# A segment-recurrent attention layer, forward and backward: folding the output projection's partial sums by block transposes on VectorE, and moving one row-maxima step behind a copy

## The chip, the cores and the metric

The kernel runs on one core of a Trainium2 chip. Its engines are named as in the profile: PE is TensorE (PEld is its weight load), DVE is VectorE, ACT is ScalarE, POOL is GpSimd, and SP is SyncE, which only waits and issues DMAs. The metric is the time of one execution on the device in microseconds, the median of several runs; lower is better.

## The reference

One layer computes `x + s * g`. With `xn = layernorm(x)` (2048 rows of 640), `g` is a gated feed-forward block, and `s` is a recurrent attention: the rows go in 64 segments of 32, and each segment sees 8 memory rows that are the attention output of the segment before.

```python
def _A_ref(x, mem0, Wq, Wk, Wv, Wo, seg_len):      # x 2048x640, 32 heads of 128, 8 memory rows
    mem = mem0
    outs = []
    for s in range(n_seg):                          # 64 segments
        xs = x[:, s * seg_len:(s + 1) * seg_len, :].copy()
        h = jnp.concatenate([mem, xs], axis=1)
        q, k, v = (jnp.einsum('btd,dhe->bhte', h, W) for W in (Wq, Wk, Wv))
        scores = jnp.einsum('bhqe,bhke->bhqk', q, k) * scale
        p = _softmax(jnp.where(mask[None, None], scores, -1000000000.0), axis=-1)
        o = jnp.einsum('bhqk,bhke->bhqe', p, v)
        o = jnp.einsum('bhte,hed->btd', o, Wo)
        mem = o[:, :M, :].copy()
        outs.append(o[:, M:, :])
    return jnp.concatenate(outs, axis=1)

xn = _layernorm(x)
out = x + _A_ref(xn, ...) * _silu(_B_ref(xn, w1, w3, w2))
_out, _vjp = jax.vjp(...)                           # the kernel returns out and the gradients of all nine inputs
```

The memory rows make the forward a chain of 64 steps, and the gradient of the memory rows makes the backward another one, from the last segment to the first.

## The kernel before, in words

The program goes through phases one after the other on one core. Two of them are recurrences, `recurrence` (forward, t = 0 to 63, about 370 to 1,580 us of the span) and `phase4_Abwd` (backward, t = 63 to 0, up to about 2,900 us). Everything around them (the projections of rows that don't depend on the memory, the feed-forward block, the weight gradients) is not touched, except for a few late DMAs.

**A step of a recurrence.** `chain(t, gap)` writes the work that depends on the step before. Between its links it calls `gap("W0")`, `gap("G1")` and so on; `FILL` (forward) and the inner `gap` (backward) put in work that doesn't hang on the chain: the full attention of earlier segments, taken three segments (a tile of 96 rows and 24 memory rows) at a time, in units of four heads (`qd`). A tile has eight units, spread over three steps as 3, 3 and 2 (`SPL`). So a forward step with t mod 3 = 0 or 1 holds three units and one with t mod 3 = 2 holds two; the first three steps hold none. `WARM` adds dummy matmuls of 128x512 at the end of some gaps. The order on each engine is exactly the written order: `in_order` ties every instruction to the one before it on its engine.

**The chain forward.** `hx` (128 x 5 x 32) holds the step's input, turned: features on partitions, five blocks of 128, and 32 columns, of which 0 to 7 are the memory rows and 8 to 31 rows that ride along. From it come K, Q and V (L306), the memory rows' scores and softmax (L647 to L674), and PV (L682), whose result is copied to `oTm` by DVE (L684) and ACT (L685). Then `packed_out` (L317) multiplies by Wo: four groups of rows of one PSUM bank (`pm`, 32 partitions each, tile positions 0, 32, 64, 96) take half of the heads (index a) and half of the 640 output columns (index b) each, so that four matmuls of 32 columns of weights run side by side. Group 2a + b holds columns 320 b to 320 b + 319, summed over the heads of half a. So the two halves over a have to be added, and the result turned back into `hx` for the next step:

- `fold_add` (L330): ACT copies partitions 64 to 127 to SBUF (`fup`, L334), DVE adds them to partitions 0 to 63 in two instructions of 160 columns (`fsum`, L336).
- `fold_turn` (L346): six PE matmuls with a selection matrix as their moving operand turn `fsum` into a PSUM bank (L352).
- a DVE copy to columns 0 to 7 of the next step's `hx` (L699 forward, L1283 backward).
- the rows are stored for later: `FS[t]` forward (a POOL DMA, L700), `GWO` backward (`fold_store`, two POOL DMAs, L343).

The next step's first matmul (Wk forward, WoT backward) waits for `hx`.

Backward, `packed_out` is called for three weights (WvT, WkT, WqT) that accumulate in the same bank, and only then the fold.

**The softmax of the units, forward.** In G2 the scores of the step's units are made (L777 to L782) and unit one's row maxima are taken (`soft_max`: L790 on DVE, then L794). In G3 come unit one's first exponentials on ACT (L812) and unit two's row maxima on DVE; both stand in front of the chain's `oTm` copies on their engines. In G4 follow the other exponentials, unit three's maxima, the products with 1/Z (`norm`: L831 on DVE, L832 on POOL) with the store of each unit's probabilities right after it (L833, a POOL DMA). In G5 and G6 PE transposes the normalised probabilities of units one and two (`turn_p`, L840), DVE copies them (L841), and unit three's `norm` follows.

**Queues.** DMAs issued from SP and from POOL stand in the written order on their engine, and each waits there for its data. SP carries nearly all loads and many stores.

Of the kernel before, what the change touches and what calls it, by code (L numbers as in the profile page):

```python
# [9 lines left out]
BF16 = mybir.dt.bfloat16  # L10
# [6 lines left out]
P = 128  # L17
# [23 lines left out]
class K:  # L41
# [109 lines left out]
    def setup_dram(self):  # L151
# [21 lines left out]
        self.FS = mk("FS", (T, 64, 320))  # L173
# [143 lines left out]
def packed_out(k, pm, x, W, first, last, i0=0, i1=16):  # L317

    nq = x.shape[2]
    for i in range(i0, i1):  # L320
        for a in range(2):
            for b in range(2):
                h = 16 * a + i
                p0 = 32 * (2 * a + b)
                k.nc.tensor.matmul(pm[p0:p0 + nq, 0:320], x[:, h, :], W[:, h, 320 * b:320 * b + 320],  # L325
                                   start=(first and i == 0), stop=(last and i == 15),
                                   tile_position=(0, p0), skip_group_check=True)


def fold_add(k, pm, pool, tag="fup"):  # L330

    fs = pool.tile([64, 320], BF16, name="fsum", tag="fsum")
    up = pool.tile([64, 320], F32, name="fup", tag=tag)
    k.nc.scalar.copy(up[:], pm[64:128, 0:320])  # L334
    for c in (0, 160):
        k.nc.vector.tensor_tensor(fs[:, c:c + 160], pm[0:64, c:c + 160], up[:, c:c + 160], ALU.add)  # L336
# [9 lines left out]
def fold_turn(k, bank, fs):  # L346

    pt = bview(bank, P, k.DC, 8)
    for (dc, p0, c0, w, b) in ((0, 0, 0, 128, 0), (3, 0, 64, 128, 1), (2, 64, 0, 64, 1), (1, 0, 128, 128, 0),
                               (4, 0, 192, 128, 1), (2, 0, 256, 64, 0)):  # L350
        kw = {} if w == 128 else dict(tile_position=(0, p0))
        k.nc.tensor.matmul(pt[p0:p0 + w, dc, :], fs[:, c0:c0 + w], k.sel[0:64, b, :], start=True, stop=True,  # L352
                           skip_group_check=True, **kw)
    return pt
# [200 lines left out]
def recurrence(k, W0, W4, Wv, Wk_, Wq, Wo, own, ps, banks):  # L555
    nc, tc = k.nc, k.tc
    D, DC, S, H, HD, T = k.D, k.DC, k.S, k.H, k.HD, k.T
    with tc.tile_pool(name="achain", bufs=1) as ch, \
# [5 lines left out]
        WARM = dict(G2=1, G3=2, G5=2)  # L564
# [33 lines left out]
        def chain(t, gap):  # L598
# [100 lines left out]
            nc.vector.tensor_copy(nxt[:, :, 0:8], pt[:])  # L699
            nc.gpsimd.dma_start(k.FS[t], fs[:])  # L700
            gap("G6")
# [121 lines left out]
        def norm(tl, qd, eng=nc.gpsimd, q=nc.gpsimd):  # L823
            n = k.geo(tl)[3]
            h0 = qd * 4
# [6 lines left out]
            eng.tensor_tensor(Pb[0:n, :, 0:n], Pb[0:n, :, 0:n], bc_last(rz[0:n], n), ALU.mult)  # L832
            q.dma_start(k.PR[tl][:, h0:h0 + 4, :], Pb[0:n])  # L833
# [84 lines left out]
        def FILL(g, t, at, kbatch):  # L918
# [164 lines left out]
def phase4_Abwd(k, out2, W0, W4, WT, own, ps, banks):  # L1083
# [7 lines left out]
    for s in range(3):  # L1091
        t0 = (2, 0, 1)[s]
        n = (T - 1 - t0 + 2) // 3
        tl0 = 1 if s == 0 else 0
        for b in range(2):
            dst = k.HRO[120 * tl0:120 * tl0 + 120 * (n - 1), :].rearrange("(t r) d -> t r d", r=120)[:, 96 + 8 * s:104 + 8 * s]
            cols = slice(320 * b, 320 * b + 320)
            later.append((dst[:, :, cols], k.FS[t0:t0 + 3 * (n - 1):3, 32 * b:32 * b + 8, :]))
            t1 = t0 + 3 * (n - 1)
            later.append((k.m_rows(k.HRO, t1 + 1)[:, cols], k.FS[t1, 32 * b:32 * b + 8, :]))  # L1100
    for b in range(2):
        later.append((k.SR[0:24 * k.NO, 320 * b:320 * b + 320].rearrange("(t r) c -> t r c", r=24),
                      k.FS[k.OT0:k.OT0 + k.NO, 32 * b + 8:32 * b + 32, :]))
    with tc.tile_pool(name="gst", bufs=1) as st, tc.tile_pool(name="gchain", bufs=1) as ch, \
# [79 lines left out]
        def chain(t, gap):  # L1184
# [93 lines left out]
            fs = fold_add(k, pm, ch, "gstg")  # L1278
            gap("G4")
            if t > 0:  # L1280
                pt = fold_turn(k, bC, fs)
                gap("G5")
                nc.vector.tensor_copy(goxs[(t - 1) % 2][:, :, 0:8], pt[:])  # L1283
            fold_store(nc.gpsimd, k.m_rows(k.GWO, t - 1) if t > 0 else out2f, fs)
# [1007 lines left out]
```

## Time and profile before

| what | value |
|---|---|
| median of 3 runs | 4698.83 us (4696.4 to 4703.39) |
| profiled execution, its own time | 4684.61 us |
| its span, first to last instruction | 4682.7 us |
| first to last fold, forward | 389 to 1,568 us, 63 folds |
| first to last turned fold, backward | 1,824 to 2,882 us, 63 folds |
| DMA share forward (450 to 1,560 us) | 0.59 |
| DMA share backward (1,824 to 2,880 us) | 0.71 |
| L334 ACT copy of 64x320 | 422 ns, x127 |
| L336 DVE add of 64x160 | 311 ns, x254 |
| L352 PE, six matmuls a fold | 177 ns each, x756 |
| L699 and L1283 DVE copy to `hx` | 199 ns, x126 |

The profile is one execution. Its page gives the busy time of each engine, then groups of instructions with their mean duration, the idle time in front of them and what ended it. A group is written as line, engine, operation, what it writes `<-` what it reads, and its count. A row of the timeline has the start in us from the span's start, the duration in us, engine, line, operation and operands, and in brackets how long the engine was idle before it and what released it; `x64` means that many instructions of one kind in a row, merged. Two instructions that are merged can overlap, so their sum is longer than the row.

### The profile page before, as it was taken

The numbers are of one execution on the slowest core, as the hardware profiler recorded it, in microseconds if no ns is written. First come the engines' busy times: TensorE is split into PE (matmuls) and PEld (weight loads), VectorE is DVE, ScalarE is ACT, GpSimd is POOL, SyncE is SP. The second block draws the span as 40 slices with busy tenths as digits, with TensorE's granted clock in tenths as the row PEclk, the third lists the DMA queues.
The fourth block names the chain that finished last, engine by engine and source line by source line (L and its number), as shares of the span: only waits on it lengthen the run. The fifth ranks groups of instructions, "written<-read, shape, count | busy, mean of one in ns | idle before, by whom it ended". The sixth has DMA issues, their size and how long they took to land. (4 is left out here: it accounts for less than half of the span.)

```text
span 4682.7 us, 159785 instructions
## 1 busy us (share of the span) xinstructions
PE 4466.5 (95%) x64504; PEld 2821.1 (60%) x64504; DVE 2244.7 (48%) x7156; ACT 1587.4 (34%) x4360; POOL 2098.4 (45%) x3528
## 2 busy tenths in 40 slices
PE   8999999999999898999999998999999999999999
PEld 4544555555555555666666665676667666666675
DVE  8734666666666534555555553343224432311460
ACT  5432555555544433333333332232223322200000
POOL 6532555555555423455444444354335533311440
PEclk9999999999999998999999999999999999999999
DMA  8773566666655677777777775664345543579783
GB/s 269 236 252 119 175 178 178 179 179 179 180 168 167 167 181 230 211 225 207 215 211 209 208 209 154 144 163 132 110 116 158 147 129 107 170 223 207 159 181 100
DMA packets 976843, 834.77 MB, mean 178 GB/s; under 512 B 518890, under 2 KB 858286, under 8 KB 974144
## 3 DMA queue, kind: packets, MB, share of 16 engines
q1 hardware_dynamic: 763879, 547.92, 42.2%
q0 software_dynamic: 129952, 228.13, 16.4%
q10 hardware_dynamic: 82275, 48.52, 4.0%
q8 instruction: 509, 8.34, 0.8%
q14 instruction: 228, 1.87, 0.1%
HBM read 472.66 MB, written 310.33 MB: 167 GB/s over the span
## 5 line engine op out<-in xcount | busy, mean ns | idle before, releaser
L1667 PE MATMUL wg<-gr,hr 128*128 128x512 bf16 x2400 | 521.7, 379 | 0.0
L1648 PE MATMUL g<-land,ghacc 128*128 128x320 bf16 x3072 | 459.9, 300 | 0.8
L1667 PEld LDWEIGHTS <-hr 128*128 128x128 bf16 x2400 | 233.9, 98 | 278.9
L306 PEld LDWEIGHTS <-hx 128*32 128x32 bf16 x10240 | 246.8, 96 | 229.1 <-issue 14.6
L1648 PEld LDWEIGHTS <-ghacc 128*128 128x128 bf16 x3072 | 289.2, 98 | 104.2 <-ACT ghacc L92 2.2
L90 DVE CAST wgo<-wg 128x512 bf16<-128x512 f32 x72 | 49.8, 692 | 471.2 <-PE wg L1667 471.2
L90 DVE CAST stg<-bank 128x512 bf16<-128x512 f32 x256 | 177.1, 692 | 158.6 <-PE bank L306 154.5
L880 POOL DMA_DIRECT2D OR<-xv x163 | 89.8, 551 | 361.1 <-ACT xv L92 338.5
L1613 POOL DMA_DIRECT2D GSP<-grs x48 | 25.5, 542 | 473.1 <-ACT grs L1605 472.0
L92 ACT COPY ghacc<-t6g 128x768 bf16<-128x768 bf16 (+1 forms) x176 | 137.1, 779 | 293.8 <-PE t6g L1630 284.5
L1324 POOL DMA_DIRECT2D VTD<-gvT x176 | 129.4, 742 | 218.7 <-ACT gvT L1323 209.5
L325 PEld LDWEIGHTS <-gkv 128*8 128x8 bf16 x8192 | 177.6, 86 | 82.2 <-issue 4.1
L832 POOL TENSOR_TENSOR xP<-xP,xrz 120x480 bf16<-120x480 bf16 x163 | 161.1, 988 | 76.0 <-DVE xrz L831 46.6
L812 ACT ACTIVATE xP<-xsp,xnm 120x120 bf16<-120x120 f32 (+1 forms) x540 | 186.1, 372 | 26.0 <-DVE xnm L794 25.9
L1654 DVE TENSOR_TENSOR ghacc<-ghacc,g 128x320 f32<-128x320 f32 x192 | 93.6, 487 | 209.9 <-PE g L1648 209.9
L336 DVE TENSOR_TENSOR fsum<-bank,fup 64x160 bf16<-64x160 f32 x254 | 69.5, 311 | 258.5 <-ACT fup L334 255.2
L92 ACT CAST wgo<-wg 128x512 bf16<-128x512 f32 x48 | 28.1, 585 | 479.8 <-PE wg L1667 407.0
L1371 POOL DMA_DIRECT2D GXP<-gks x157 | 91.0, 580 | 189.5 <-ACT gks L1369 188.8
L325 PE MATMUL bank<-Wo,oTm 128*32 128x320 bf16 x4032 | 154.2, 307 | 18.4 <-DVE oTm L684 18.4
L325 PE MATMUL bank<-WkT,gkv 128*8 128x320 bf16 x4096 | 162.8, 299 | 4.2 <-issue 2.2
L325 PE MATMUL bank<-WvT,gkv 128*8 128x320 bf16 x4096 | 166.4, 305 | 0.5 <-DVE gkv L1197 0.5
L306 PE MATMUL bank<-Wq,hx 128*32 128x512 bf16 x2560 | 161.6, 381 | 0.0
(389 smaller groups left out, 10916.1 us busy)
## 6 DMA issues: line engine op xcount, KB each, us to landing
QVS<-stg SPq DMA_DIRECT2D x128, 256.0 KB
kT<-VTD SPq DMA_DIRECT2D x64, 320.0 KB
PR<-xP POOLq DMA_DIRECT2D x168, 120.0 KB, 3.1
VTD<-gvT POOLq DMA_DIRECT2D x168, 120.0 KB, 4.0
land<-DSR SPq DMA_DIRECT2D x168, 120.0 KB
land<-PR SPq DMA_DIRECT2D x168, 120.0 KB
OR<-xv POOLq DMA_DIRECT2D x163, 120.0 KB, 3.0
orr<-OR SPq DMA_DIRECT2D x14, 1280.0 KB
```

What stands on the lines that cost most here:

```text
L90: return nc.vector.tensor_copy(out, in_)
L92: return nc.scalar.copy(out, in_)
L306: k.nc.tensor.matmul(bank[32 * g:32 * g + 32, :], x[:, dc, :], W[:, dc, c0:c0 + 512], start=(dc == 0), stop=(dc == k.DC - 1), tile_positio ...
L325: k.nc.tensor.matmul(pm[p0:p0 + nq, 0:320], x[:, h, :], W[:, h, 320 * b:320 * b + 320], start=(first and i == 0), stop=(last and i == 15), ...
L812: nc.scalar.activation(Pb[0:n, j, 0:n], sp[0:n, j, :], ACT.Exp, bias=nmx[0:n, j:j + 1], scale=k.scale, accum_out=Z[0:n, j:j + 1])
L832: eng.tensor_tensor(Pb[0:n, :, 0:n], Pb[0:n, :, 0:n], bc_last(rz[0:n], n), ALU.mult)
L880: q.dma_start(k.OR[120 * tl:120 * tl + n, c0:c0 + 512], v[0:n])
L1324: nc.gpsimd.dma_start(k.VTD[tl][:, :, h0:h0 + 4, :], vTq[:])
L1371: (nc.sync if (tl, qd) in pro else nc.gpsimd).dma_start(k.GXP[tl, :, qd, 0:ns], ks[:].rearrange("p s i h m -> p s i (h m)"))
L1648: nc.tensor.matmul(pg[:], ring[:, i, j, r0:r0 + P], Ws[qd][i][:, j, 320 * h:320 * h + 320], start=(i == 0 and j == 0), stop=(i == 2 and j ...
L1654: nc.vector.tensor_tensor(a, a, pg[:], ALU.add)
L1667: nc.tensor.matmul(pw[:], hr[:, tl, dc * P:(dc + 1) * P], grs[i][:, tl, :], start=(tl == 0), stop=(tl == NF - 1))
```

## The change

The two output column halves are no longer 320 wide blocks but interleaved blocks of 32: the columns are taken as 20 blocks of 32, and group b gets every second one. Each matmul still has 320 columns, read from the weights as ten runs of 32.

`fold_add` and `fold_turn` become one function `fold`. ACT copies partitions 64 to 127 in two halves (the even and the odd ones of the group's ten blocks), and DVE adds each half, the even one to partitions 0 to 63 and the odd one to partitions 64 to 127 of a tile of 128 x 160. With this arrangement a transpose of every 32x32 block (one DVE instruction over 128 x 160) leaves features on partitions and rows on columns, in the order that `hx` has; a DVE copy takes the 8 memory columns of each block to `hx`. The six matmuls go, and with them the use of bank C.

`FS` changes from (T, 64, 320) to (T, 32, D). The stores of FS and GWO go from POOL to SP and become four DMAs each, of runs of 32 columns (64 bytes); forward, the store of FS stands behind the loads of gap G5. The late copies out of FS (`later`) become nine DMAs instead of sixteen.

In the forward, gap G6 is merged into G5, so that unit two's transposes and unit three's `norm` follow G5's work, and one WARM matmul of G5 is dropped, the other stands behind them. Unit two's row maxima move from G3 to the head of G4, behind the `oTm` copy. The store of unit one's probabilities moves behind unit two's product.

```diff
-        self.FS = mk("FS", (T, 64, 320))
+        self.FS = mk("FS", (T, 32, D))
...
     for i in range(i0, i1):
         for a in range(2):
+            h = 16 * a + i
+            w = W[:, h, :].rearrange("p (j b r) -> p b j r", b=2, r=32)
             for b in range(2):
-                h = 16 * a + i
                 p0 = 32 * (2 * a + b)
-                k.nc.tensor.matmul(pm[p0:p0 + nq, 0:320], x[:, h, :], W[:, h, 320 * b:320 * b + 320],
+                k.nc.tensor.matmul(pm[p0:p0 + nq, 0:320].rearrange("p (j r) -> p j r", r=32), x[:, h, :], w[:, b],
                                    start=(first and i == 0), stop=(last and i == 15),
                                    tile_position=(0, p0), skip_group_check=True)
...
+def fold(k, pm, pool, dst, tag="fup"):
+
+    ft = pool.tile([P, 2, 160], BF16, name="fsum", tag="fsum")
+    fs, tr = ft[:, 0], ft[:, 1]
+    up = pool.tile([64, 2, 160], F32, name="fup", tag=tag)
+    v = pm[:, 0:320].rearrange("p (c s r) -> p s c r", s=2, r=32)
+    rows = lambda ap: ap.rearrange("p (c r) -> p c r", r=32)
+    for s in range(2):
+        k.nc.scalar.copy(rows(up[:, s]), v[64:128, s])
+        k.nc.vector.tensor_tensor(rows(fs[64 * s:64 * s + 64]), v[0:64, s], rows(up[:, s]), ALU.add)
+    if dst is not None:
+        k.nc.vector.transpose(tr, fs)
+        k.nc.vector.tensor_copy(dst, tr.rearrange("p (c m) -> p c m", m=32)[:, :, 0:8])
     return fs
...
 def fold_store(eng, dst, fs):
 
-    for b in range(2):
-        eng.dma_start(dst[:, 320 * b:320 * b + 320], fs[32 * b:32 * b + 8, :])
+    n = dst.shape[0]
+    d = dst.rearrange("m (c g r) -> g m c r", g=4, r=32)
+    for g in range(4):
+        eng.dma_start(d[g], fs[32 * g:32 * g + n, :].rearrange("m (c r) -> m c r", r=32))
...
-        WARM = dict(G2=1, G3=2, G5=2)
+        WARM = dict(G2=1, G3=2, G5=1)
...
             packed_out(k, pm, oTm, Wo, True, True)
-            fs = fold_add(k, pm, ch)
+            fs = fold(k, pm, ch, hxs[(t + 1) % 2][:, :, 0:8])
             gap("G5")
-            pt = fold_turn(k, bC, fs)
-            nxt = hxs[(t + 1) % 2]
-            nc.vector.tensor_copy(nxt[:, :, 0:8], pt[:])
-            nc.gpsimd.dma_start(k.FS[t], fs[:])
-            gap("G6")
+            fold_store(nc.sync, k.FS[t], fs)
...
-            q.dma_start(k.PR[tl][:, h0:h0 + 4, :], Pb[0:n])
+            if q is not None:
+                norm_store(tl, qd, q)
+
+        def norm_store(tl, qd, q=nc.gpsimd):
+            n = k.geo(tl)[3]
+            q.dma_start(k.PR[tl][:, 4 * qd:4 * qd + 4, :], xPs[qd % 3][0:n])
...
             elif g == "G3":
                 at(lambda a, b: soft_exp(a, b, 0, 2), t, 0)
+            elif g == "G4":
                 at(soft_max, t, 1)
-            elif g == "G4":
                 at(lambda a, b: soft_exp(a, b, 2, 4), t, 0)
                 at(lambda a, b: soft_max(a, b, True), t, 2)
-                at(norm, t, 0)
+                at(lambda a, b: norm(a, b, q=None), t, 0)
...
                 at(soft_exp, t, 1)
-                at(norm, t, 1)
+                at(lambda a, b: norm(a, b, q=None), t, 1)
+                for i in range(2):
+                    at(norm_store, t, i)
                 at(soft_exp, t, 2)
             elif g == "G5":
...
-            elif g == "G6":
                 at(turn_p, t, 1)
                 at(norm, t, 2)
...
-            fs = fold_add(k, pm, ch, "gstg")
+            fs = fold(k, pm, ch, goxs[(t - 1) % 2][:, :, 0:8] if t > 0 else None, "gstg")
             gap("G4")
-            if t > 0:
-                pt = fold_turn(k, bC, fs)
-                gap("G5")
-                nc.vector.tensor_copy(goxs[(t - 1) % 2][:, :, 0:8], pt[:])
-            fold_store(nc.gpsimd, k.m_rows(k.GWO, t - 1) if t > 0 else out2f, fs)
+            gap("G5")
+            fold_store(nc.sync, k.m_rows(k.GWO, t - 1) if t > 0 else out2f, fs)
             gap("G6")
```

More of the change, by code (lines that the diff above doesn't have):

```diff
@@ L327, in packed_out @@
                                    tile_position=(0, p0), skip_group_check=True)
[L330 to L336, printed above, removed]
+def fold(k, pm, pool, dst, tag="fup"):
[10 more added lines that the diff above has]
+        k.nc.vector.tensor_copy(dst, tr.rearrange("p (c m) -> p c m", m=32)[:, :, 0:8])
@@ L337, in fold_add @@
     return fs
 def fold_store(eng, dst, fs):
-    for b in range(2):
-        eng.dma_start(dst[:, 320 * b:320 * b + 320], fs[32 * b:32 * b + 8, :])
[L346 to L354, printed above, removed]
+    n = dst.shape[0]
@@ L694, in chain @@
             packed_out(k, pm, oTm, Wo, True, True)
-            fs = fold_add(k, pm, ch)
+            fs = fold(k, pm, ch, hxs[(t + 1) % 2][:, :, 0:8])
             gap("G5")
-            pt = fold_turn(k, bC, fs)
-            nxt = hxs[(t + 1) % 2]
-            nc.vector.tensor_copy(nxt[:, :, 0:8], pt[:])
-            nc.gpsimd.dma_start(k.FS[t], fs[:])
-            gap("G6")
+            fold_store(nc.sync, k.FS[t], fs)
         WT = {}
@@ L824, in norm @@
             n = k.geo(tl)[3]
-            h0 = qd * 4
             Pb = xPs[qd % 3]
@@ L1094, in phase4_Abwd @@
         tl0 = 1 if s == 0 else 0
[L1095 to L1103, printed above, removed]
+        dst = k.HRO[120 * tl0:120 * tl0 + 120 * (n - 1), :].rearrange("(t r) d -> t r d", r=120)[:, 96 + 8 * s:104 + 8 * s]
+        later.append((dst, k.FS[t0:t0 + 3 * (n - 1):3, 0:8, :]))
+        t1 = t0 + 3 * (n - 1)
+        later.append((k.m_rows(k.HRO, t1 + 1), k.FS[t1, 0:8, :]))
+    later.append((k.SR[0:24 * k.NO, :].rearrange("(t r) c -> t r c", r=24), k.FS[k.OT0:k.OT0 + k.NO, 8:32, :]))
     with tc.tile_pool(name="gst", bufs=1) as st, tc.tile_pool(name="gchain", bufs=1) as ch, \
```

## The prediction

> **What bounds the kernel now.** I read part 1 of the page first, then the groups of instructions, then the timeline of one step of each recurrence, last SP's own instructions.
>
> ```profile
> PE 4466.5 (95%) x64504; PEld 2821.1 (60%) x64504; DVE 2244.7 (48%) x7156; ACT 1587.4 (34%) x4360; POOL 2098.4 (45%) x3528
> ```
>
> PE looks full, but in the two recurrences part of this is filler: WARM matmuls and whatever the gaps put between two links of a chain. What sets a step is that chain, so I look at the end of a step, forward, t = 45:
>
> ```profile
> 1246.97 0.17 DVE L794 TENSOR_SCALAR xnm<-xmx 120x4 f32<-120x4 f32 x1
> 1247.05 0.29 DVE L684 CAST oTm<-bank 128x128 bf16<-128x128 f32 x1
> ...
> 1247.48 2.36 PE L325 MATMUL bank<-Wo,oTm 128*32 128x320 bf16 x64 [0.29 <-DVE oTm L684]
> ...
> 1247.77 0.38 ACT L812 ACTIVATE xP<-xsp,xnm 120x120 bf16<-120x120 f32 x1
> ...
> 1248.33 0.98 POOL L832 TENSOR_TENSOR xP<-xP,xrz 120x480 bf16<-120x480 bf16 x1 [1.36 <-issue]
> ...
> 1249.11 0.62 ACT L808 ACTIVATE xP<-xsp 120x480 bf16<-120x480 f32 x1
> ...
> 1249.94 0.42 ACT L334 COPY fup<-bank 64x320 f32<-64x320 f32 x1 [0.21 <-PE bank L325]
> ...
> 1250.20 1.00 POOL L832 TENSOR_TENSOR xP<-xP,xrz 120x480 bf16<-120x480 bf16 x1
> 1250.40 0.55 DVE L336 TENSOR_TENSOR fsum<-bank,fup 64x160 bf16<-64x160 f32 x2 [0.85 <-ACT fup L334]
> ...
> 1250.77 0.78 PE L352 MATMUL bank<-sel,fsum 64*128 64x8 bf16 x6
> ...
> 1251.49 0.38 PE L840 MATMUL xpp<-ident,xP 120*128 120x120 bf16 x4
> ...
> 1251.59 0.20 DVE L699 CAST hx<-bank 128x40 bf16<-128x40 f32 x1 [0.33 <-PE bank L352]
> ...
> 1251.85 2.34 PE L306 MATMUL bank<-Wk,hx 128*32 128x512 bf16 x40
> ```
>
> Call e the end of the output projection (1247.48 + 2.36 = 1249.84). From e to the next step's first projection are 2.01 us: ACT copy, two adds, six turning matmuls, hx copy. PE fills them, but no link is shortened by that. Backward the same chain stands almost bare (e = 2214.40):
>
> ```profile
> 2214.45 0.42 ACT L334 COPY fup<-bank 64x320 f32<-64x320 f32 x1 [2.26 <-PE bank L325]
> 2214.91 0.55 DVE L336 TENSOR_TENSOR fsum<-bank,fup 64x160 bf16<-64x160 f32 x2 [2.87 <-ACT fup L334]
> ...
> 2215.28 0.78 PE L352 MATMUL bank<-sel,fsum 64*128 64x8 bf16 x6 [0.56 <-DVE fsum L336]
> ...
> 2216.10 0.20 DVE L1283 CAST hx<-bank 128x40 bf16<-128x40 f32 x1 [0.65 <-PE bank L352]
> ...
> 2216.45 1.26 PE L306 MATMUL bank<-WoT,hx 128*32 128x512 bf16 x20
> ```
>
> 2.05 us from e. There are 63 such places in each recurrence, mean periods 18.98 us (389.30 to 1566.13, 62 steps) and 17.03 us.
>
> **What the Trainium skill says.** "VectorE: DVE Perf Modes", section "The three transpose paths", prices a VectorE transpose of 128x128 bf16 at 311 ns, blocks of 32x32 only; the kernel before has none. The same page, "Two Vector instructions with no wait between them", says that an instruction whose output starts in another quadrant of partitions than the last output waits for all earlier ones; today both adds write from partition 0 and overlap (0.55 us for two of 0.311), the new ones write from 0 and from 64, so I take no overlap. "SBUF — State Buffer", "Door 1: The DMA port swizzle", says that reads stay at full bandwidth while successive accesses fall in one 16-byte line; the new projection reads runs of 32 bf16, 64 bytes. The trace agrees as far as it goes: the score matmuls of L782 read three runs of 32 columns and take 202 ns, the contiguous 96-column transposes of L1630 205. The same page, "Who interferes with whom", says that a VectorE copy from SBUF to SBUF in a two-port mode and a GpSimd operation block each other; the DVE copies of L641, which run beside POOL's, have a median of 283 ns and a maximum of 664.
>
> **The change part by part.**
>
> Fold, backward. Gone from the chain are the turning matmuls (first add's end to their end 0.84 us, 2215.22 to 2216.06) and the wait behind them. New: two ACT copies of 64x160. From L334 (422 ns for 320) and the 128x128 copy of L685 (262 ns) ACT pays 0.83 ns an element, so 0.29 each, overlapping by 0.09 as successive ACT operations here do. In us after e: copies 0.05-0.34 and 0.25-0.54, adds 0.37-0.69 and 0.72-1.03 (0.31 each, 0.03 from engine to engine), transpose of 160 columns from 1.06: 0.311 plus 32 more columns at 0.96 GHz, an estimate of 0.345, to 1.41; copy 128x40, 0.19 (today's from PSUM takes 0.199), to 1.63; then 0.14 to the matmul as today (hx ends 2216.30, WoT starts 2216.45): 1.77 against 2.05. 0.27 us x 63 = 17.0. PE holds dprob, one WARM and gmem in the gap, under 1.2 us together, and is free. The DVE work of unit three (L1353 and before) follows the hx copy and moves with it, as do the copies of the next projection. Bounds: a transpose at two elements a cycle (0.26), or half as long again (0.52); a copy of 0.15 to 0.25; that gives 0.05 to 0.40 us, 3 to 25 in all.
>
> Row maxima, forward. L684 starts at e-2.79 behind L790 and L794 of unit two, while PV's matmuls ended at e-3.09; they release a reader in 0.10, so it can start at e-2.99. The other half (ACT L685, 1246.94 + 0.26) ends at e-2.64 and now decides: the projection starts 0.14 earlier, as far behind as today behind L684. The price: unit two's maxima (0.66) and L794 (0.17) come behind the copy. Row maxima end e-1.95, L794 e-1.75, and the exponentials of unit two start at e-1.66 instead of e-2.07; ACT ends L808 at e+0.30 instead of e-0.11.
>
> Fold, forward, same step. fup now waits for ACT and not for PE: copies 0.21-0.50 and 0.41-0.70, adds 0.53-0.85 and 0.88-1.19, transpose to 1.57, copy to 1.79, Wk at 1.85, against 2.01: 0.16. The other route to Wk is unit two's turn (L840), which now stands before it on PE: its 1/Z at 0.16, POOL's product to 1.31 (its neighbour's PR store no longer stands between), transposes 1.37, then 0.22 for them and 0.21 for the one WARM: 1.80, also in time. At t mod 3 = 1 the reduce runs into the copy instead of following 0.09 later, everything is 0.18 sooner, and Wk starts at 1.67 instead of 2.01. At t mod 3 = 2 there is no third unit: PE is free at 1.68, hx ready at 1.60, gain 0.33. With 20 steps of each, 20 x (0.16 + 0.34 + 0.33) = 16.6, and 0.26 for each of the first three: 17.4. Bounds from the same durations: 4 to 27. Unit one's transposes (L840) come late at t mod 3 = 0, at 0.12 instead of -0.07; nothing but filler follows. The WARM that goes (0.21) lies in that filler.
>
> Stores. FS and GWO leave POOL (0.55 and 2 x 0.53 per step) for SP, as four DMAs each of 64-byte runs. SP's similar DMAs of L1273 take 0.63 each, so 2.5 us of SP per step.
>
> ```profile
> 2699.31 0.94 SPq L1311 DMA_DIRECT2D xP<-PR  x1
> 2700.76 0.34 SPq L1215 DMA_DIRECT2D GOS<-gstg  x1
> ...
> 2709.28 1.25 SPq L1273 DMA_DIRECT2D DSR<-dSm  x2
> ```
>
> Backward they go in at 2700.25, where SP has half a microsecond free; the list behind (GOS, three unit loads, VTD, PM, QM, KS) comes some 2 us later and catches up by 2709.28, since SP waits about 0.7 and 0.9 us on the way. SP issues 12.0 us of a 17.0 us step; with these 14.5, with gaps near 16. The loads delayed serve the next step or a later one, over 10 us away: nothing. Forward SP is about half used; the KS store behind is delayed by up to 0.3 us and nobody near waits. The 64-byte packets are small in number beside the rest. Fewer FS reads later (9 for 16 on POOL): nothing. PR's later store: read only backward, nothing.
>
> Sum: 17.0 + 17.4 = 34.4 us. Against the profiled execution's own time, 4684.61 (span 4682.7): 4650.2. The shown runs' median is 4698.83, 14.2 above it; the saving is the same there: 4664.4, so 4664.
>
> **Rivals.**
> A, the softmax gives the forward gain back: exponentials and POOL's product of unit two (0.98 to 1.00 us, started once its 1/Z is there) end later than I reckon and L840 holds Wk. For it: at t mod 3 = 0 the two routes are 0.05 apart. Against: POOL has lost a 0.57 us store in between. Then only the backward gain stays: 4682.
> B, SP is full in the backward: 16 of 17 us, and the gride transposes (1.26 us on SP every fourth step) don't fit. For it: 71% use today. Against: slack of a whole step. If half a microsecond a step is lost, 31 of 34 us go: 4695, no change.
> C, the projection slows with its interleaved columns. L325's 64 matmuls take 2.36 us, 36.9 ns apart, four running at once; b = 0 and 1 now read neighbouring 64-byte runs instead of runs 640 bytes apart. There are 16,320. From 2.1 ns each on (34.4/16,320), the gain is gone; at 3.7 (a tenth) 60 us come on: 4698.83 - 34.4 + 60 = 4724, slower. Against: L782, above.
> D, the hx copy is held by POOL: up to a store's 0.55 us at each of 126 places, 69 us: 4734, slower. Against: the copy starts as POOL's product ends, and L641's median.
>
> **How the numbers follow.** Forecast 0.68, A 0.14, B 0.06, C 0.08, D 0.04. The bounds add up to a gain of 7 to 52 us, 4647 to 4692; since both low ends together are unlikely I close it at 4688, with A inside; B, C, D, 0.18, stay outside. 0.2%, 9.4 us, is what a measurement of this kernel can tell from no change. Faster: forecast and A, 0.82, less a little for their weak end: 0.81. Same 0.08 (B and that end), slower 0.11.
>
> **What would show it.** Right: Wo and WkT matmuls of L325 still 2.36 us for 64; from e to WoT about 1.77 us, to Wk 1.67 to 1.85; the projection 0.14 earlier behind PV; a transpose near 0.345 us and no L352. Wrong: a longer L325; a wait of the hx copy for POOL, or of PE at L840 for POOL longer than at Wk; waits of PE for loads in the backward; a period not below 17.0 us there.

## The result and the profile after

The changed kernel takes 4744.2 us (median of 4 runs, 4732.7 to 4747.5), the kernel before 4701.1 us beside it (4696.4 to 4703.9): a ratio of 1.0088, 95% interval 1.0069 to 1.0108. It is slower by about 0.9%, some 40 us. The profiled execution took 4744.95 us (span 4743.0) against 4684.61 (4682.7).

Where the span grew is read by cutting it at the ends of the output projections (63 folds in each recurrence):

| stretch | before, us | after, us |
|---|---|---|
| start to the first forward fold | 389.3 | 390.1 |
| first to last forward fold (62 steps) | 1176.8 | 1177.9 |
| between the recurrences | 257.7 | 259.8 |
| first to last backward fold (62 steps) | 1056.1 | 1114.5 |
| what is left behind it | 1802.7 | 1800.6 |

All of the loss is in the backward, and in the forward nothing was gained. Part 1 of the page, the line that answers to the first one shown of before:

```profile
PE 4352.1 (92%) x63403; PEld 2768.7 (58%) x63684; DVE 2289.4 (48%) x7282; ACT 1618.4 (34%) x4487; POOL 1980.3 (42%) x3330
```

PE lost 114 us of busy time while the span grew by 60: the turning matmuls and a WARM are gone, and PE now waits more. DVE has 45 us more (transposes, and adds that no longer overlap).

The chain, first backward. The projection ends at e = 2263.18. The timeline of that step (start, duration, engine, line, operation, operands, and in brackets the idle time before it and what ended it):

```profile
2263.23 0.29 ACT L339 COPY fup<-bank 64x160 f32<-64x160 f32 x1 [1.88 <-PE bank L326]
...
2263.55 0.32 DVE L340 TENSOR_TENSOR fsum<-bank,fup 64x160 bf16<-64x160 f32 x1 [2.73 <-ACT fup L339]
...
2263.90 0.29 ACT L339 COPY fup<-bank 64x160 f32<-64x160 f32 x1 [0.38 <-DVE fsum L340]
...
2264.22 0.32 DVE L340 TENSOR_TENSOR fsum<-bank,fup 64x160 bf16<-64x160 f32 x1 [0.35 <-ACT fup L339]
...
2264.57 0.34 DVE L342 STREAM_TRANSPOSE fsum<-fsum 128x160 bf16<-128x160 bf16 x1
...
2264.95 0.17 DVE L343 COPY hx<-fsum 128x40 bf16<-128x40 bf16 x1
...
2265.27 2.34 PE L306 MATMUL bank<-WoT,hx 128*32 128x512 bf16 x40 [1.31 <-DVE hx L343]
```

Every duration is as reckoned to 0.02 us, but copy, add, copy, add run strictly one after the other: the second ACT copy, which needs nothing from DVE, is released by DVE's first add. So WoT starts 2.09 us after e, where it was 2.05.

The step at t = 45, forward, e = 1251.18, in the timeline:

```profile
1248.38 0.29 DVE L682 CAST oTm<-bank 128x128 bf16<-128x128 f32 x1 [0.68 <-PE bank L680]
...
1248.82 2.36 PE L326 MATMUL bank<-Wo,oTm 128*32 128x320 bf16 x64
...
1250.88 0.58 ACT L801 ACTIVATE xP<-xsp 120x480 bf16<-120x480 f32 x1
...
1251.49 0.29 ACT L339 COPY fup<-bank 64x160 f32<-64x160 f32 x1
1251.57 0.98 POOL L824 TENSOR_TENSOR xP<-xP,xrz 120x480 bf16<-120x480 bf16 x1 [0.23 <-issue]
...
1252.16 0.29 ACT L339 COPY fup<-bank 64x160 f32<-64x160 f32 x1 [0.38 <-DVE fsum L340]
...
1252.61 0.38 PE L837 MATMUL xpp<-ident,xP 120*128 120x120 bf16 x4 [0.62 <-POOL xP L824]
...
1253.22 0.17 DVE L343 COPY hx<-fsum 128x40 bf16<-128x40 bf16 x1
1253.45 2.34 PE L306 MATMUL bank<-Wk,hx 128*32 128x512 bf16 x40 [0.45 <-DVE hx L343]
```

The copy `oTm` is now released by PE and not by DVE's row maxima, the projection still takes 2.36 us for 64 matmuls, and unit two's transposes (L837) are done before `hx`. But ACT's exponentials end at e + 0.28, the fold begins at e + 0.31, the same wait for the first add stands inside it, and Wk starts 2.27 us after e (2.01 before).

The backward steps. Most keep a period near 17.03 us, but 12 of the 62 take 19 to 24 us, nine of these right behind a step in which SP also issued a gride transpose (a DMA that loads `gride` turned, L270, every fourth step). SP's own instructions in one of them (a step of 23.0 us, begun at 2605.78) and the end of the step before, from the timeline:

```profile
2594.19 2.99 SPq L352 DMA_DIRECT2D GWO<-fsum  x4
2597.29 1.28 SPq L270 DMA_TRANSPOSE gride<-GS  x1
...
2608.65 1.28 SPq L1267 DMA_DIRECT2D DSR<-dSm  x2
2610.03 0.57 SPq L1168 DMA_DIRECT2D xp<-GXP  x1
2610.70 0.64 SPq L1298 DMA_DIRECT2D kT<-QVM  x1
2611.39 0.61 SPq L265 DMA_DIRECT2D kT<-QVX  x1
2612.09 0.54 SPq L265 DMA_DIRECT2D kT<-GOS  x1
2612.72 0.38 SPq L1302 DMA_DIRECT2D xP<-PR  x1
...
2615.39 2.95 SPq L352 DMA_DIRECT2D GWO<-fsum  x4
2618.45 0.39 SPq L1209 DMA_DIRECT2D GOS<-gstg  x1
```

From 2610.03 on, in the rows left out too, SP goes from one DMA to the next within 0.04 to 0.11 us: it waits for nothing. Four stores and a transpose in the step before have pushed its list back, and the unit loads of this step are issued while the step's own units already stand on PE. The waits of this step (engine and line, what for, us in total, times, longest):

```profile
DVE gOst L1215 <- PE bank L1214: 4.8, 1, 4.8
...
PE gvpt L1311 <- DMA kT<-QVX: 3.5, 1, 3.5
```

PE, which works in written order, stood 3.5 us at a unit's first matmul (L1311, at 2614.68) for the load of QVX that SP issued at 2611.39 and that landed at 2614.63, and the chain's transposes (L1214) stand behind that matmul. Over the whole backward the rows of this wait are:

```profile
PE gvpt L1311 <- DMA kT<-QVS: 18.8, 9, 4.3
PE gvpt L1311 <- DMA kT<-QVX: 10.5, 6, 3.5
```

In the kernel before, PE waits there once, for 0.3 us.

### The profile page after: what moved, and what is told of

The parts are those of the page before. It is cut to its first block, busy times and chain, and to the rows that moved or that the text cites. A ratio compares the mean times of both kernels' runs of the same rounds, so it can differ in the third digit from the quotient of the medians.

```text
span 4743.0 us, 158663 instructions
## 1 busy us (share of the span) xinstructions
PE 4352.1 (92%) x63403; PEld 2768.7 (58%) x63684; DVE 2289.4 (48%) x7282; ACT 1618.4 (34%) x4487; POOL 1980.3 (42%) x3330
## 4 chain that ended last, share of the span: by engine, by line
PE 72%; DVE 9%; DMA 8%; ACT 5%; issue 3%; SPq 1%; POOL 0%; ACTq 0%; DVEq 0%; another core or an unknown queue 0%; POOLq 0%
PE bank L306 11%; PE wg L1658 11%; PE bank L326 11%; PE g L1639 8%; PE oa L1805 4%; PE wa L2193 2%; PE b0pb L364 2%; PE r6p L1589 2%; PE t6g L1621 2%; DVE fsum L340 2%; ACT xP L805 2%; PE pgxb L2126 2%; ACT fup L339 1%; PE bank L1220 1%; PE bank L314 1%
## 5 line engine op out<-in xcount | busy, mean ns | idle before, releaser
L306 PE MATMUL bank<-WoT,hx 128*32 128x512 bf16 x2560 | 153.6, 386 | 91.7 <-DVE hx L343 91.7
L340 DVE TENSOR_TENSOR fsum<-bank,fup 64x160 bf16<-64x160 f32 x254 | 80.5, 317 | 262.2 <-ACT fup L339 260.8
L326 PE MATMUL bank<-WvT,gkv 128*8 128x320 bf16 x4096 | 184.0, 328 | 0.9 <-DVE gkv L1191 0.9
L306 PE MATMUL bank<-Wk,hx 128*32 128x512 bf16 x2560 | 153.1, 386 | 32.2 <-DVE hx L343 31.8
L245 POOL DMA_DIRECT2D land<-GOS x256 | 146.7, 578 | 37.6 <-PE bank L306 9.4
```

The lines of the kernel that those rows point to most:

```text
L245: eng.dma_start(d, src if src.shape[0] > 1 else src[0])
L306: k.nc.tensor.matmul(bank[32 * g:32 * g + 32, :], x[:, dc, :], W[:, dc, c0:c0 + 512], start=(dc == 0), stop=(dc == k.DC - 1), tile_positio ...
L326: k.nc.tensor.matmul(pm[p0:p0 + nq, 0:320].rearrange("p (j r) -> p j r", r=32), x[:, h, :], w[:, b], start=(first and i == 0), stop=(last ...
L340: k.nc.vector.tensor_tensor(rows(fs[64 * s:64 * s + 64]), v[0:64, s], rows(up[:, s]), ALU.add)
```

## The experiments

Two theories. S: the stores of GWO fill SP in the backward, the unit loads come late, and that is the loss. F: the fold costs the time. Inside the fold, two readings of the wait: T, the two copies share a tile; K, ACT and DVE read one PSUM bank and are put in order. In the table, "backward" is the stretch of 62 steps from the first to the last fold of the profiled execution, which is 1056.1 us in the kernel before.

| run | ratio to before | 95% interval | backward, us |
|---|---|---|---|
| changed kernel | 1.0088 | 1.0069 to 1.0108 | 1114.5 |
| GWO stores on POOL | 1.0006 | 0.9999 to 1.0013 | 1063.2 |
| one ACT copy, stores on SP | 1.0085 | 1.0070 to 1.0100 | 1117.8 |
| one ACT copy, stores on POOL | 0.9975 | 0.9965 to 0.9984 | 1051.5 |
| the same, row maxima back in G3 | 0.9967 | 0.9957 to 0.9978 | 1055.1 |
| the same, FS on POOL too | 0.9976 | 0.9968 to 0.9985 | 1056.5 |
| one ACT copy, stores on ACT | 1.0017 | 1.0007 to 1.0028 | 1090.7 |
| two tiles for the copies | 1.0100 | 1.0071 to 1.0129 | 1120.0 |
| two banks forward, stores on POOL | 0.9962 | 0.9952 to 0.9973 | 1064.9 |
| before, 2 GWO stores on SP | 1.0007 | 0.9997 to 1.0018 | 1061.6 |
| before, 4 stores on SP | 1.0029 | 1.0019 to 1.0040 | 1072.8 |
| before, 8 stores on SP | 1.0148 | 1.0131 to 1.0166 | 1138.1 |
| before, row maxima moved alone | 0.9991 | 0.9982 to 1.0000 | 1056.5 |

The kernel before lay at 4696 to 4706 us beside these runs, so runs are compared by their ratios; 0.1% is 4.7 us. A stretch of a single profile varies by some us: the changed kernel and that with two tiles, whose folds take equally long, differ by 6 us forward (1177.9 and 1171.6) and by 5 backward.

**GWO stores back on POOL.**

```diff
-            fold_store(nc.sync, k.m_rows(k.GWO, t - 1) if t > 0 else out2f, fs)
+            fold_store(nc.gpsimd, k.m_rows(k.GWO, t - 1) if t > 0 else out2f, fs)
```

> The changed kernel, with the backward's four GWO stores of a step put back on POOL; fold and forward as changed. Theory S (SP is full in the backward: 2.5 us a step more to issue, unit loads come late): the backward steps of 20 to 23 us go, the 63 backward steps take 1022 to 1028 us in the profile instead of 1079.8, and the time falls by 50 to 60 us, to about 4685 to 4697. Theory F (the fold itself costs the time, SP's delays are hidden): no more than 5 us fall, 4739 to 4746. If POOL in its turn is late with four DMAs, something between.

4698.6 us. The time goes back to that of the kernel before, and the backward falls by 51 us in the profile (the expectation's stretch ends two folds sooner; in it this run took 1028.8 us, 1022.6 before, 1079.8 in the changed kernel). By the ratios the move is worth 0.0082, 39 us; by the two medians, taken at different times, 46. That is short of the 50 to 60 expected, and a few longer steps stay (five over 18 us; three before, 14 in the changed kernel). PE's waits for QVS and QVX at the units' first matmuls are gone as well (none over 0.1 us). So the same four DMAs a step, with the same runs of 64 bytes, don't cost this time when POOL issues them. S holds, F falls: what remains of the whole change with these stores elsewhere is no gain and no loss.

**One ACT copy for both halves.**

```diff
-    up = pool.tile([64, 2, 160], F32, name="fup", tag=tag)
+    up = pool.tile([64, 320], F32, name="fup", tag=tag)
...
+    u = up[:].rearrange("p (c s r) -> p s c r", s=2, r=32)
+    k.nc.scalar.copy(up[:], pm[64:128, 0:320])
...
     for s in range(2):
-        k.nc.scalar.copy(rows(up[:, s]), v[64:128, s])
-        k.nc.vector.tensor_tensor(rows(fs[64 * s:64 * s + 64]), v[0:64, s], rows(up[:, s]), ALU.add)
+        k.nc.vector.tensor_tensor(rows(fs[64 * s:64 * s + 64]), v[0:64, s], u[:, s], ALU.add)
```

> The changed kernel, with one ACT copy of 64x320 in the fold ahead of both adds instead of two halves that alternate with the adds; GWO stores stay on SP. From the durations measured: copy 0.05-0.47 after the projection's end, adds to 1.18, transpose to 1.56, hx copy to 1.77, next matmul at about 1.91 instead of 2.10 backward, and about 2.1 instead of 2.27 forward. If the ACT copy waits for the add because both read one PSUM bank, this gains 0.15 to 0.2 us a fold: forward 9 to 12 us. Backward theory S says that SP sets many steps, so less than the 12 us there: time 4720 to 4738. Theory F (fold alone) says all of 20 to 25: 4719 to 4724, with backward steps as long as before wherever no fold is late.

4732.2 us, a ratio that cannot be told from that of the changed kernel. The trace shows why: forward the stretch of 62 steps fell from 1177.9 to 1165.7 us, about the 9 to 12 us expected. Backward each fold is 0.18 us shorter and the usual steps fell from 17.03 to 16.9 us, but the stretch didn't fall (1117.8 for 1114.5): the long steps, which are there as before (13 over 19 us, 12 in the changed kernel), took the gain.

**Both together.** The two edits above in one kernel.

> Both: one ACT copy, and GWO stores on POOL. Theory S and the bank order together: 60 us from the stores and 20 to 24 from the fold: 4662 to 4685, faster than the kernel before (about 4700). If only the stores matter: 4685 to 4697. If neither: 4740.

4680.6 us, faster than the kernel before, as expected. Against the run with stores on POOL alone the copy is worth 0.0031, 15 us. The backward fold of this kernel in the timeline (e = 2224.16):

```profile
2224.21 0.42 ACT L338 COPY fup<-bank 64x320 f32<-64x320 f32 x1 [1.88 <-PE bank L326]
2224.67 0.67 DVE L341 TENSOR_TENSOR fsum<-bank,fup 64x160 bf16<-64x160 f32 x2 [2.86 <-ACT fup L338]
2225.37 0.34 DVE L343 STREAM_TRANSPOSE fsum<-fsum 128x160 bf16<-128x160 bf16 x1
2225.75 0.17 DVE L344 COPY hx<-fsum 128x40 bf16<-128x40 bf16 x1
2226.07 2.13 PE L306 MATMUL bank<-WoT,hx 128*32 128x512 bf16 x36 [1.12 <-DVE hx L344]
```

WoT at e + 1.91 (expected 1.91), 0.14 before that of the kernel before; the usual periods went from 17.03 to 16.89 us.

**Row maxima put back.** That kernel with unit two's row maxima in G3 again.

```diff
             elif g == "G3":
                 at(lambda a, b: soft_exp(a, b, 0, 2), t, 0)
+                at(soft_max, t, 1)
             elif g == "G4":
-                at(soft_max, t, 1)
```

> As the run with one ACT copy and GWO stores on POOL, but with unit two's row maxima back in G3, in front of the attention output's copy. The trace of the changed kernel shows PV's end to the projection 0.73 to 0.53 us, 0.2 us in 40 steps that have a unit two in them with a turn on the path: 8 to 12 us slower than that run. If the softmax of unit two is what ends the step at t mod 3 = 0, the move gives nothing there: 3 to 6 us. If the move costs more behind the copy than it gains ahead of it: faster by some us.

4678.7 us: not slower by 8 to 12 us, nor by 3 to 6; the two intervals overlap. The timeline at t = 45, first with the maxima moved (e = 1239.94), ACT's queue:

```profile
1239.65 0.58 ACT L802 ACTIVATE xP<-xsp 120x480 bf16<-120x480 f32 x1
...
1240.26 0.42 ACT L338 COPY fup<-bank 64x320 f32<-64x320 f32 x1
```

and with the maxima back in G3 (e = 1245.91):

```profile
1245.19 0.62 ACT L802 ACTIVATE xP<-xsp 120x480 bf16<-120x480 f32 x1
...
1246.02 0.42 ACT L338 COPY fup<-bank 64x320 f32<-64x320 f32 x1 [0.20 <-PE bank L326]
```

With the move, the last exponentials end at e + 0.29 and hold the fold's copy to e + 0.32; without it ACT is idle and waits for PE (e + 0.11). So part of what the projection gains in front is paid back behind it: Wk starts at e + 2.08 with the move and at e + 1.94 without it (medians). By the medians of the forward steps the move still wins, by 0.26, 0.11 and 0.07 us at t mod 3 = 0, 1 and 2, some 9 us over 60 steps; the times don't show this, and what the move is worth in this kernel stays open.

**Row maxima alone on the kernel before**, the same lines moved there, nothing else.

> The kernel before with one edit: unit two's row maxima behind the copy of the attention output. My prediction's step said the projection starts 0.14 us earlier and unit two's exponentials end 0.41 us later. With the old fold, the copy of the fold waits for ACT until 0.30 us after the projection's end instead of starting at 0.10, so 0.2 is lost at t mod 3 = 0 and 1 and 0.14 to 0.2 gained everywhere: sum about 0 to 5 us faster, 4691 to 4698. Rival: PE's turn of unit two moves behind the fold anyway and all 60 steps gain 0.14 to 0.2: 8 to 12 us faster, 4684 to 4688. Other rival: the softmax is the bound and the step gets longer: 4700 to 4712.

4696.0 us beside 4701.0: some 4 us faster by the ratio, with an interval from 0 to 8.5. That fits the expected 0 to 5; the first rival's 8 to 12 is only touched at its end. In the profile the steps with t mod 3 = 0 are 0.20 us shorter (median 18.66 to 18.46), the other two kinds 0.20 and 0.17 longer, and the forward stretch is 7 us longer (1183.5, 1176.8 before). So the profile doesn't show where 4 us could come from; gains and losses nearly cancel.

**FS stores on POOL too.** `fold_store(nc.sync, k.FS[t], fs)` becomes `fold_store(nc.gpsimd, k.FS[t], fs)` in the kernel with the maxima back.

> One ACT copy in the fold, GWO stores on POOL, row maxima in G3 (4678.7 us), and now the forward's four FS stores on POOL too. If the forward's SP has room, as the prediction said, there is nothing to gain, and POOL, where the stores stand among the products with 1/Z, may hold unit three's product or the late copies by up to 2.4 us a step, on nobody's path: 4674 to 4690. If FS on SP costs time as GWO does: 5 to 20 us faster, 4659 to 4674.

4687.0 us, ratio 0.9976 where it was 0.9967: no gain. So forward the stores on SP cost nothing that these runs show.

**Which part of the stores fills SP: their number, their runs, or their place.** The kernel before, GWO moved to SP, as 2, 4 and 8 DMAs:

```diff
     for b in range(2):
-        eng.dma_start(dst[:, 320 * b:320 * b + 320], fs[32 * b:32 * b + 8, :])
+        for c in range(0, 320, 80):
+            eng.dma_start(dst[:, 320 * b + c:320 * b + c + 80], fs[32 * b:32 * b + 8, c:c + 80])
...
-            fold_store(nc.gpsimd, k.m_rows(k.GWO, t - 1) if t > 0 else out2f, fs)
+            fold_store(nc.sync, k.m_rows(k.GWO, t - 1) if t > 0 else out2f, fs)
```

(the form with eight; the form with four has `c in (0, 160)`, that with two leaves the loop as it was).

> The kernel before, with its two GWO stores of a backward step issued on SP instead of POOL, nothing else. It has the old fold, contiguous runs of 640 bytes and two DMAs. Theory S (the number of DMAs that SP has to issue): 1.1 to 1.3 us more on SP a step, 12.0 to about 13.2 of 17.0; spikes only at the steps with the gride transposes: 5 to 25 us slower than before, 4702 to 4722. Theory P (short packets of 64 bytes cost the time, wherever they are issued): no change, 4690 to 4702.

> The kernel before, with its GWO rows stored by four DMAs of 8x160 (runs of 320 bytes) on SP. Same bytes, same fold, but the issue count of the changed kernel. Theory S: 2.4 to 2.8 us more on SP a step, backward steps of 20 to 23 us at the gride transposes, 40 to 57 us slower than before: 4737 to 4754. Theory P: no more than 5 us slower, up to 4703. If a place in SP's list behind the fold is what counts and not the number, this and the run with two stores come out alike.

> The kernel before, with its GWO rows stored by eight DMAs of 8x80 (runs of 160 bytes) on SP. Measured so far: a GWO DMA takes SP 0.286 us with one run a row, 0.285 with runs of 320 bytes, 0.688 with five runs of 64 bytes a row; SP's issuing per backward step is 11.98 us before, 12.68 with two stores (no change in time), 13.38 with four (12 us slower), 14.80 in the changed kernel (46 us slower than with its stores on POOL). Theory S (only SP's issuing time counts): eight times 0.29 gives 14.3 us a step, and 25 to 45 us over the kernel before: 4721 to 4741. Theory R (the 160 short runs a step cost, in the DMA queues and not in SP's time; here there are 64): no more than a little over the run with four, 4703 to 4716.

4697.5, 4708.7 and 4770.8 us. The place behind the fold alone costs nothing (two stores: ratio 1.0007). Four cost 14 us by the ratio, not the 40 to 57 expected, because a DMA of long runs is cheaper to issue than I had put it. SP's rows of the stores of one step, with two, with four, and with eight:

```profile
2105.18 0.64 SPq L343 DMA_DIRECT2D GWO<-fsum  x2
```

```profile
2114.44 1.30 SPq L344 DMA_DIRECT2D GWO<-fsum  x4
```

```profile
2191.68 3.00 SPq L344 DMA_DIRECT2D GWO<-fsum  x8
```

Four of the changed kernel's DMAs took 2.95 us, as much as eight of these. Eight long-run stores then cost 70 us by the ratio; R (short runs cost in the queues) had at most 4716 and falls. So a kernel without a new fold and without a 64-byte run in these stores loses as much as the changed one, and more, once they take SP as long. In its backward PE waits 39.5 us at the units' first matmuls, where the two rows of the changed kernel make 29.3. Why it loses some 30 us more than the stores of the changed kernel at an equal length of the row, and more than the 25 to 45 us expected, stays open. One candidate, not tested, is that SP itself waits at these stores for earlier loads to land:

```profile
SPq L344 <- DMA xP<-PR: 11.5, 25, 2.1
SPq L344 <- DMA kT<-QVS: 5.7, 7, 2.5
```

At the changed kernel's stores SP waits for a load once, 0.2 us. Adding up SP's DMAs with the pauses under 0.15 us between them over the first 61 backward steps of each profile:

| kernel | SP taken per step, us | mean step, us |
|---|---|---|
| before | 13.5 | 17.0 |
| 2 on SP | 14.4 | 17.1 |
| 4 on SP | 15.3 | 17.3 |
| 8 on SP | 16.4 | 18.4 |
| changed | 16.8 | 18.0 |

The first microsecond cost nothing that can be measured, the later ones did. (The figures per step in the expectations, 11.98 to 14.80, leave the pauses out and are sums over 61 steps divided by 62; rightly divided they are 12.2 to 15.0.)

**Stores on ACT's queue**, with one ACT copy: `fold_store(nc.scalar, ...)` for GWO.

> One ACT copy in the fold, and the four GWO stores issued on ACT's own queue; row maxima as changed. With POOL's queue this was 4680.6 us, with SP's 4732. Theory S: SP is as free as in the run with POOL, and ACT has about 2.5 us to spare after the fold before the copy of the next projection's second half: 4668 to 4684. If issuing on ACT holds that copy (four times 0.5 to 0.7 us ahead of it in ACT's order), each backward step loses up to 1 us: 4690 to 4740.

4705.0 us: the second expectation. One backward step of its timeline, ACT's queue:

```profile
2377.48 0.67 ACTq L353 DMA_DIRECT2D GWO<-fsum  x1
...
2378.19 2.15 ACTq L353 DMA_DIRECT2D GWO<-fsum  x3
2380.93 0.59 ACT L92 CAST gstg<-bank 128x512 bf16<-128x512 f32 x1 [3.12 <-DMA GWO<-fsum]
```

The copy of the next projection's second half stands behind the stores. But the usual periods are those of the run with POOL (16.89 us), and the loss is again in single long steps (up to 22 us), with SP as free as before (13.4 us a step, pauses counted). Over the backward ACT waits at this copy for a store 83.2 us in 25 places, and PE waits 10.0 us at the units' first matmuls. How much of the 20 us against POOL's queue comes from this copy and how much from something else isn't settled.

**What the second copy waits for.** First T: each half copy gets a tile of its own in the changed kernel.

```diff
-    up = pool.tile([64, 2, 160], F32, name="fup", tag=tag)
+    ups = [pool.tile([64, 160], F32, name="fup", tag=tag), pool.tile([64, 160], F32, name="fup1", **more)]
...
-        k.nc.scalar.copy(rows(up[:, s]), v[64:128, s])
+        k.nc.scalar.copy(rows(ups[s][:]), v[64:128, s])
...
```

> The changed kernel, with the two ACT copies of a fold in two tiles of their own; the copies still alternate with the adds, stores stay on SP. Theory T (the second copy waits for the first add because both use one tile): the wait goes, fold 0.3 us shorter, as predicted at first: 15 to 25 us faster than the changed kernel, 4719 to 4729. Theory K (it waits because ACT and DVE read one PSUM bank, which are put in order): the wait stays, next matmul at 2.10 us backward as before, time 4737 to 4748.

4742.8 us. The row of the waits, in the changed kernel and in this one:

```profile
ACT fup L339 <- DVE fsum L340: 48.6, 127, 0.5
```

```profile
ACT fup L339 <- DVE fsum L340: 48.7, 127, 0.5
```

127 folds, 0.38 us each, in both. T falls. Then K, in the kernel with stores on POOL: forward, the sums of the second half of the heads go to bank C.

```diff
+                po = pm2 if a and pm2 is not None else pm
-                k.nc.tensor.matmul(pm[p0:p0 + nq, 0:320].rearrange("p (j r) -> p j r", r=32), x[:, h, :], w[:, b],
+                k.nc.tensor.matmul(po[p0:p0 + nq, 0:320].rearrange("p (j r) -> p j r", r=32), x[:, h, :], w[:, b],
...
-        k.nc.scalar.copy(rows(up[:, s]), v[64:128, s])
+        k.nc.scalar.copy(rows(up[:, s]), v2[64:128, s])
...
-            packed_out(k, pm, oTm, Wo, True, True)
+            packed_out(k, pm, oTm, Wo, True, True, pm2=bC)
...
```

> The changed kernel with GWO stores on POOL (4698.6 us) and alternating half copies, where forward the two halves over the heads are summed in two PSUM banks: partitions 0 to 63 in the bank as before, 64 to 127 in bank C, which the new fold had freed. ACT then reads one bank and DVE the other. Theory K (the second ACT copy waits for the first add because both read one bank): forward the wait goes, the hx copy starts 0.2 to 0.35 us earlier (2.03 to about 1.75 after the projection's end at t mod 3 = 0 and 1, 1.83 to about 1.6 at 2), and 63 folds give 10 to 18 us: 4681 to 4689; backward, where nothing is edited, the wait stays, 64 times. If the wait stays forward as well, it is neither the tile nor the bank: 4694 to 4703. If two banks cost the projection its 2.36 us: slower than that.

4686.3 us beside 4705.7, the lowest ratio of all, 0.9962. Its row of the waits:

```profile
ACT fup L341 <- DVE fsum L342: 24.5, 64, 0.4
```

64 waits, the backward ones, where nothing was edited. Forward they are gone, in the timeline at t = 45 (e = 1240.90):

```profile
1241.21 0.48 ACT L341 COPY fup<-bank 64x160 f32<-64x160 f32 x2
1241.53 0.67 DVE L342 TENSOR_TENSOR fsum<-bank,fup 64x160 bf16<-64x160 f32 x2 [0.37 <-ACT fup L341]
...
1242.23 0.34 DVE L344 STREAM_TRANSPOSE fsum<-fsum 128x160 bf16<-128x160 bf16 x1
1242.34 0.38 PE L839 MATMUL xpp<-ident,xP 120*128 120x120 bf16 x4 [0.63 <-POOL xP L826]
1242.61 0.18 DVE L345 COPY hx<-fsum 128x40 bf16<-128x40 bf16 x1
...
1242.87 2.34 PE L306 MATMUL bank<-Wk,hx 128*32 128x512 bf16 x40
```

The two copies now overlap (0.48 us for two of 0.29), and Wk starts at e + 1.97 instead of 2.27. Forward 62 steps took 1163.2 us instead of 1178.9. K holds: what orders the two reads goes by the bank.

This run and the three with one ACT copy and POOL stores beat both kernels; they differ from one another by less than their intervals. Two banks forward with one copy backward was not tried together.

## Why the prediction was wrong

**Stores: "The loads delayed serve the next step or a later one, over 10 us away: nothing."** This step failed, and it is what made the kernel slower: 0 was put, 39 us came (1.0088 against 1.0006; 51 us in the profiled backward). The distance was wrong already in the kernel before. Of the 157 units that PE begins in its backward stretch, 65 had their load (QVX or QVS) issued less than 10 us ahead of their first matmul, the nearest 3.9 us. One of them, in the timeline of before:

```profile
2560.66 0.61 SPq L265 DMA_DIRECT2D kT<-QVX  x1
...
2565.57 0.37 PE L1320 MATMUL gvpt<-ident,kT 120*128 120x120 bf16 x4
```

That is 4.9 us. The same unit in the changed kernel is the one shown above, with 3.3 us from issue to matmul, and the load took 3.2 us of it to land. With less than 4 us there is one unit before and there are 12 after.

The sum on SP was too small as well: "14.5, with gaps near 16" came out as 15.0, and 16.8 with the pauses. SP's own DMAs took 12.2 us a step and not 12.0; the four stores take 2.95 us from the first to the last, and not 2.5 (the neighbour's 0.63 a DMA stood for 0.69); and the pauses make 1.8 us a step. And the list that "catches up by 2709.28" was read in a step without a gride transpose. By an estimate from these numbers, a step with one needs about 13.2 + 2.95 + 1.3 us, which is past 17 (13.2 is the 13.5 of the kernel before, less its quarter of a transpose). Then the unit loads, which stand behind the stores on SP, come too late for PE.

**Rival B** named this place and this mechanism and put its price at "half a microsecond a step", 31 us, with a chance of 0.06. The rival was right in its mechanism and its size was too small: 39 us came. It should have been the large case: I had 16 of 17 us in my own text, and reckoned the overflow as a mean per step, where it comes as late loads that make one step out of five 2 to 6 us longer.

**Fold: "copies 0.05-0.34 and 0.25-0.54".** The first holds to 0.01; the second ran from 0.72 to 1.01. This is the second step that failed: with the GWO stores back on POOL nothing is left of the 34 us of gain (1.0006); by the ratios one copy brings 15 us back and two banks forward 21. The term that failed is the overlap of the two copies "as successive ACT operations here do": between them stands DVE's add of the same bank. All else follows with the right durations: adds 0.32 (0.31 put), transpose 0.345 on average over 126 (0.345 put, from the 311 ns that the Trainium skill, "VectorE: DVE Perf Modes", "The three transpose paths", gives for 128 columns), hx copy 0.17 to 0.18 (0.19). Backward WoT at 2.09 instead of 1.77: 17.0 us of gain became a loss of 0.04 a fold. Forward the fold's gain of 17.4 became 1.1 us of loss over 62 steps, the row maxima's gain included; with two banks 13.6 of the 17.4 are there (1176.8 to 1163.2, in single profiles). That the new adds don't overlap was put in and holds: in the kernel with one ACT copy, where the second add waits for no other engine, two take 0.67 us; before, where both wrote from partition 0, they took 0.55. This agrees with the section "Two Vector instructions with no wait between them" of the same page, by which an output that starts in another quadrant than the last one makes an instruction wait for all earlier ones.

**Row maxima: "the projection starts 0.14 earlier", exponentials of unit two later by 0.41.** Both are there: from PV's end to the projection 0.74 us before, 0.54 after (median of 63), and the exponentials end at e + 0.28 for the 0.30 put. The price was rightly seen too: the fold's copy waits for ACT. The net worth is a few us at most in the runs, and they don't settle it.

**Rivals A, C, D.** A: the turn of unit two ends 0.23 us before `hx` starts to be copied, so it isn't what holds Wk; in the kernel with two banks it ends at 1242.72, 0.07 us before the copy's end, as close as the text said. C: 64 matmuls in 2.36 us, as before; interleaved columns cost nothing. D: the hx copy has a mean of 182 ns, and DVE's idle time in front of all 126 is 4.8 us.

## What to carry to other kernels

A queue that only issues is an engine with a busy share of its own: count its DMAs with the pauses between them, in the fullest step and not in the mean one, before putting anything more on it. Price a DMA by its runs as well as by its bytes. And before calling a delayed load harmless, read from the trace, for every load behind, how far ahead of its first use it is issued. Where two engines take turns at one PSUM bank, draw the order between their reads too: two halves that look like a pipeline can be a chain. When a change does several things, one of them can undo the rest: here the versions with the GWO stores left on POOL, and with one copy or two banks, are 0.24 to 0.38% faster than before.

## What the runs showed of the hardware that was not expected

- SP's time for a store went with the number of runs and not with the bytes: 8 rows in 8 runs of 640, 320 or 160 bytes took 0.285 to 0.286 us (medians in three kernels), 8 rows of five runs of 64 bytes each (40 runs) 0.688 us. From these two that is an estimate of 13 ns for each further run. On POOL the difference is small: 0.532 us for 8 runs of 640 bytes, 0.592 for 40 of 64.
- ACT's read of partitions 64 to 127 and DVE's of 0 to 63 of one bank come one after the other, 127 times of 127; in two banks they don't. The Trainium skill, "PSUM — Partial Sum Buffer", section "PSUM bank collisions raise a hardware error", says that two engines may use different quadrants (32 partitions) of one bank at once, as these do. In the traces the second ACT copy waits for the semaphore that DVE's add raises, and with two banks the forward copy has no such wait. So the order seen here is one that the program carries; no run here took it away within one bank.
- SP's mean load doesn't give the cost: with SP taken 14.4 us of a step of 17.1 nothing was lost that can be measured, 15.3 cost 14 us in all, 16.4 cost 70 and 16.8 about 40. The loss came as single long steps.
